# Softmax sums of a pair of slots: multiplied by a constant on VectorE instead of ScalarE

## The chip, the cores and the metric

The kernel runs on one core of a Trainium2 chip. A core has a matrix engine (TensorE, in the profile PE, its weight loads PEld), three engines for element-wise work (VectorE = DVE, ScalarE = ACT, GpSimd = POOL) and a queue for DMA transfers (SyncE = SP). Each engine works through its own instructions in order and waits on semaphores for the others. SBUF is the working memory with 128 partitions, PSUM the small memory into which TensorE writes. The metric is the device time of one execution in microseconds (us), the median of several.

## The reference

The reference is one transformer block with a conditioning vector `c`: a layer norm modulated by `c`, attention over the last 512 positions of a cached K and V, a second modulated layer norm and a gated GELU network.

```python
W = min(4096, max(256, Sk // 4))              # 512
q = (x @ wq).reshape(B, Sq, Hq, Dh)           # 2048 rows, 32 heads of 128
k = k_cache[:, :, Sk - W:, :]                 # 8 heads, each used by 4 heads of q
scores = einsum("bhqd,bhkd->bhqk", q, k) * Dh ** -0.5
p = softmax(scores, axis=-1)
o = einsum("bhqk,bhkd->bhqd", p, v)
A = o.reshape(B, Sq, Hq * Dh) @ wo
x = x + ga * A
x = x + gb * ((gelu(h @ w_gate) * (h @ w_up)) @ w_down)
```

The part that matters here is the softmax: for each row of 512 scores the kernel takes the maximum, the exponentials, their sum, and the exponentials divided by the sum.

## The kernel before

Every matrix operand is held as two float16 halves (a high part and the rest), and every product is three matmuls (`mm3`, its matmuls are line 91), which gives nearly float32 precision from float16 matmuls.

The attention runs first, as 512 slots `t`. A slot is 128 rows of q of one head against the 512 keys. Four slots make a unit (one head, 512 rows). The loop over `t` writes the instructions of every engine in the order in which they are to run; no scheduler changes it. What belongs to one tile of scores is spread over several slots:

- slot t: `scores(t)`, three matmuls into one of two PSUM banks `ps`; `peak(t)` (L1000, VectorE), the negated row maximum `nm`; `expo(t)` (L1009, ScalarE), the exponentials `ee`, with their row sum going to one column of the tile `sm` through a second small instruction that reads the accumulator. `sm` has two columns, one for each slot of a pair (an even slot and the odd one behind it).
- odd slot, behind its `expo`: `recips(t - 1)` (L1014, ScalarE) copies the two sums of the pair, times 1/PSC with PSC = 2**15, into a tile `rr`.
- the even slot after that, behind its `peak` and behind what `run(("e", t))` holds (the low half of a q tile or of an attention output, L754): the inversion `rr = 1/rr` (L1017, VectorE).
- slot t + 2: `high` (L1021, ScalarE), the float16 high half `p` = ee * rr; slot t + 3: `low` (L1026, VectorE), p's low half = ee * rr - high, which reads two tiles of SBUF, and the transposing DMA of both halves into `pt`, from which the product with v (`po`) reads two units later.

The scores of slot t + 2 need the bank `ps` of slot t, so TensorE waits there until `expo(t)` has read it. Between these stand, on TensorE, the projections of q for the next unit (`qa`, `qb`, `qc`, in the first units `pq`), the products with v (`po`) and with wo (`py`). VectorE also adds up q's partial products (L781), makes low halves (L754) and accumulates the output (L970); ScalarE also makes high halves (L753), copies PSUM (L903) and takes sums of squares (L220). GpSimd scales and splits weights (L161, L162, L165, L816 and others). After the 512 slots comes the feed-forward network, in which no softmax stands.

The helper `ts` (L186) is VectorE's tensor_scalar with one operation. All small tiles named here are 128 x 2 or 128 x 1 float32 in SBUF; `ee` is in SBUF in all but 18 of the slots.

Of the kernel before, what the change touches and what calls it, by code (L numbers as in the profile page):

```python
# [14 lines left out]
AF = mybir.ActivationFunctionType  # L15
# [15 lines left out]
PSC = 2.0 ** 15  # L31
# [34 lines left out]
def block_kernel(ctx: ExitStack, tc: tile.TileContext, x, kT, v, wq, wo, wg, wu, wd, cT, wc, wm, out):  # L66
    nc = tc.nc
# [116 lines left out]
    def ts(out, src, a, b=None, op0=ALU.mult, op1=ALU.mult):  # L184
        if b is None:
            nc.vector.tensor_scalar(out, src, a, None, op0=op0)  # L186
        else:
            nc.vector.tensor_scalar(out, src, a, b, op0=op0, op1=op1)  # L188
# [429 lines left out]
    qT, pT, oT, E = {}, {}, {}, {}  # L618
# [392 lines left out]

    def recips(t):
        r = small.tile([P, 2], F32, name="rr", bufs=4)
        nc.scalar.activation(r, E[t]["sm"], AF.Copy, scale=1.0 / PSC)  # L1014
        for k in range(2):
            E[t + k]["r"] = r[:, k:k + 1]
        return lambda: nc.vector.reciprocal(r, r)  # L1017

    def high(t):
        p16 = pool.tile([P, 2, W], F16, tag="p16", name="p16", bufs=NP16)  # L1020
# [553 lines left out]
    with tc.manual_schedule():  # L1574
        begin()
        nexty, invs = [], {}
        for t in range(T + TAIL):
# [21 lines left out]
            if t < T:  # L1599
                expo(t)  # L1600
                if t % 2:
                    invs[t + 1] = recips(t - 1)
# [253 lines left out]
```

## Time and profile before

| | us |
|---|---|
| median of three runs | 1729.17 (1729.11 to 1729.21) |
| profiled execution, its own time | 1728.67 |
| its span, first to last instruction | 1726.9 |

| engine | busy, us | share of the span | instructions |
|---|---|---|---|
| TensorE, matmuls | 1708.5 | 99% | 7999 |
| VectorE | 1425.5 | 83% | 2481 |
| ScalarE | 1256.6 | 73% | 2823 |
| GpSimd | 1089.2 | 63% | 1322 |

A row of a group of instructions reads: line, engine, operation, tiles out and in with their shapes, count; then busy time in us and mean length of one in ns; then the idle time in front of them and what ended it. In the view of one line the three numbers are the shortest, median and longest length in ns. A row of waits reads: who waited for whom, then us in total, number of waits, longest. A row of the timeline reads: start in us from the span's start, length in us, engine, line, operation, tiles; in square brackets stands idle time of the engine in front of it and what ended it. A row of a stretch reads: from and to, its length, then for each engine the busy time and its instructions, TensorE's granted clock as a share of full speed, the DMA share and GB/s. A matmul of 512 columns shows as some 0.38 us, but the next one starts 0.22 us after it, since they overlap.

### The profile page before, as it was taken

The numbers are of one execution on the slowest core, as the hardware profiler recorded it, in microseconds if no ns is written. First come the engines' busy times: TensorE is split into PE (matmuls) and PEld (weight loads), VectorE is DVE, ScalarE is ACT, GpSimd is POOL, SyncE is SP. The second block draws the span as 40 slices with busy tenths as digits, with TensorE's granted clock in tenths as the row PEclk, the third lists the DMA queues.
The fourth block names the chain that finished last, engine by engine and source line by source line (L and its number), as shares of the span: only waits on it lengthen the run. The fifth ranks groups of instructions, "written<-read, shape, count | busy, mean of one in ns | idle before, by whom it ended". The sixth has DMA issues, their size and how long they took to land.

```text
span 1726.9 us, 26328 instructions
## 1 busy us (share of the span) xinstructions
PE 1708.5 (99%) x7999; PEld 784.1 (45%) x8001; DVE 1425.5 (83%) x2481; ACT 1256.6 (73%) x2823; POOL 1089.2 (63%) x1322
## 2 busy tenths in 40 slices
PE   7999999999999999999999999999999999999999
PEld 4444444444444444444444444444444444444444
DVE  8888898988888899888888888888896788676666
ACT  7988788888888877888777777787785354455442
POOL 3879777776788884655665755747760345735424
PEclk9999999999999999999999999999999999999999
DMA  7999999999999998989999999999997555365353
GB/s 245 215 207 214 210 215 199 231 203 223 214 223 225 209 209 182 215 207 228 209 222 223 211 227 209 199 220 222 223 232 163 163 147 192 123 165 174 97 157 104
DMA packets 693454, 343.51 MB, mean 199 GB/s; under 512 B 579136, under 2 KB 602688, under 8 KB 693312
## 3 DMA queue, kind: packets, MB, share of 16 engines
q1 hardware_dynamic: 693024, 341.30, 86.0%
q8 instruction: 63, 1.03, 0.3%
q14 instruction: 79, 0.65, 0.1%
q10 hardware_dynamic: 288, 0.52, 0.1%
HBM read 137.50 MB, written 63.70 MB: 117 GB/s over the span
## 4 chain that ended last, share of the span: by engine, by line
PE 91%; ACT 4%; DVE 3%; DMA 1%; issue 1%; SPq 0%; DVEq 0%; ACTq 0%
PE py L91 19%; PE po L91 17%; PE ps L91 17%; PE qa L91 8%; PE fa L91 8%; PE fc L91 4%; PE qc L91 4%; PE ya L91 3%; PE qb L91 2%; PE fb L91 2%; PE yc L91 2%; ACT ee L1009 1%; PE yb L91 1%; DVE nm L1000 1%; ACT p L1021 1%
## 5 line engine op out<-in xcount | busy, mean ns | idle before, releaser
L1009 ACT ACTIVATE ee<-ps,nm 128x512 f32<-128x512 f32 x512 | 349.6, 683 | 185.4 <-DVE nm L1000 182.6
L1026 DVE SCALAR_TENSOR_TENSOR p<-ee,rr,p 128x512 f16<-128x512 f32 x512 | 457.8, 894 | 8.8 <-ACT p L1021 8.2
L1000 DVE TENSOR_REDUCE nm<-ps 128x1 f32<-128x512 f32 x512 | 349.7, 683 | 94.7 <-PE ps L91 92.5
L91 PE MATMUL ps<-k,qt 128*128 128x512 f16 x1536 | 415.3, 379 | 4.7 <-ACT ee L1009 3.6
L1021 ACT ACTIVATE p<-ee,rr 128x512 f16<-128x512 f32 x512 | 363.9, 711 | 18.8 <-DVE rr L1017 11.6
L91 PE MATMUL po<-pt,v 128*128 128x512 f16 x1536 | 372.9, 379 | 0.7 <-DVE nm L1000 0.7
L91 PE MATMUL py<-wo,ot 128*128 128x512 f16 x1536 | 371.3, 379 | 0.0
L91 PEld LDWEIGHTS <-w 128*128 128x128 f16 x2184 | 213.8, 98 | 260.2 <-issue 2.9
L91 PEld LDWEIGHTS <-v 128*128 128x128 f16 x1536 | 150.1, 98 | 182.4 <-issue 1.6
L91 PEld LDWEIGHTS <-ot 128*128 128x128 f16 x1536 | 150.2, 98 | 181.3
L91 PEld LDWEIGHTS <-qt 128*128 128x128 f16 x1536 | 145.8, 98 | 176.1 <-issue 3.9
L1333 POOL TENSOR_TENSOR fg<-fg 128x512 f32<-128x512 f32 x48 | 63.0, 1312 | 136.0 <-DVE fg L1307 133.1
L754 DVE SCALAR_TENSOR_TENSOR ot<-po,ot 128x512 f16<-128x512 f32 x128 | 87.8, 686 | 41.3 <-ACT ot L753 41.1
L1317 ACT ACTIVATE at<-fg 128x512 f16<-128x512 f32 x92 | 56.4, 626 | 77.2 <-DVE fg L1307 60.7
L1009 ACT ACTIVATION_READ_ACCUMULATOR ee<-ps,nm 128x1 f32 x512 | 100.2, 196 | 0.0
L970 DVE SCALAR_TENSOR_TENSOR acc<-py,ysc,acc 128x512 f32<-128x512 f32 x128 | 94.6, 739 | 5.3 <-PE py L91 5.3
L91 PE MATMUL qa<-t,w 128*128 128x512 f16 x348 | 84.9, 379 | 0.0
L91 PE MATMUL fa<-t,w 128*128 128x512 f16 x336 | 81.6, 379 | 0.1
L237 POOL TENSOR_TENSOR lw<-lw,half__86 128x1 f32<-128x1 f32 x38 | 26.2, 690 | 86.4 <-DVE lw L188 86.3
L404 POOL TENSOR_TENSOR rs<-rs,nhalf 128x1 f32<-128x1 f32 x32 | 18.5, 577 | 93.8 <-DVE rs L398 85.9
L753 ACT ACTIVATE ot<-po 128x512 f16<-128x512 f32 x128 | 73.9, 578 | 5.1 <-PE po L91 5.1
L1703 DVE SCALAR_TENSOR_TENSOR yt<-ya,dyc,yt 128x512 f32<-128x512 f32 x82 | 60.3, 745 | 19.5 <-PE ya L91 19.5
(258 smaller groups left out, 2799.8 us busy)
## 6 DMA issues: line engine op xcount, KB each, us to landing
w<-kept SPq DMA_DIRECT2D x123, 256.0 KB, 3.2
wo<-kept SPq DMA_DIRECT2D x72, 256.0 KB, 3.2
kept<-stage SPq DMA_DIRECT2D x67, 256.0 KB, 3.3
raw<-in_wo SPq DMA_DIRECT2D x56, 256.0 KB, 3.2
kept<-w SPq DMA_DIRECT2D x39, 256.0 KB, 3.4
rw<-in_wq SPq DMA_DIRECT2D x38, 256.0 KB, 3.2
hs<-hf SPq DMA_DIRECT2D x32, 256.0 KB, 2.9
pt<-p SPq DMA_TRANSPOSE x512, 3.5
```

The costliest lines, as they stand in the source:

```text
L91: nc.tensor.matmul(ps, a, b, start=first and n == 0, stop=last and n == 2, skip_group_check=chain)
L237: nc.gpsimd.tensor_tensor(out, out, half_, op=ALU.pow)
L753: nc.scalar.activation(t[:, 0, :], src, AF.Copy, scale=scale)
L754: return lambda: nc.vector.scalar_tensor_tensor(t[:, 1, :], src, scale, t[:, 0, :], op0=ALU.mult, op1=ALU.subtract)
L970: nc.vector.scalar_tensor_tensor(acc[ti], st["p"], by, acc[ti], op0=ALU.mult, op1=ALU.add)
L1000: nc.vector.tensor_reduce(nm, E[t]["ps"], axis=AX.X, op=ALU.max, negate=True)
L1009: nc.scalar.activation(e, E[t]["ps"], AF.Exp, bias=E[t]["nm"], scale=1.0, accum_out=sm[:, t % 2:t % 2 + 1])
L1021: nc.scalar.activation(p16[:, 0, :], E[t]["e"], AF.Copy, scale=E[t]["r"])
L1026: nc.vector.scalar_tensor_tensor(p16[:, 1, :], E[t]["e"], E[t]["r"], p16[:, 0, :], op0=ALU.mult, op1=ALU.subtract)
L1317: nc.scalar.activation(t[:, 0, :], g, AF.Copy)
L1333: nc.gpsimd.tensor_tensor(g[o], g[a], g[b], op=ALU.subtract)
L1703: nc.vector.scalar_tensor_tensor(YT[key], ps, by, YT[key], op0=ALU.mult, op1=ALU.add)
```

## The change

The operation of ScalarE in `recips` goes. In its place, VectorE multiplies the two sums by 1/PSC in front of the inversion, where the inversion stood already.

```diff
     def recips(t):
         r = small.tile([P, 2], F32, name="rr", bufs=4)
-        nc.scalar.activation(r, E[t]["sm"], AF.Copy, scale=1.0 / PSC)
+        sm = E[t]["sm"]
         for k in range(2):
             E[t + k]["r"] = r[:, k:k + 1]
-        return lambda: nc.vector.reciprocal(r, r)
+
+        def inverse():
+            ts(r, sm, 1.0 / PSC)
+            nc.vector.reciprocal(r, r)
+
+        return inverse
```

The lines behind it move by five: `high` is L1026 and `low` L1031 in the kernel after, the inversion L1020. On VectorE, around the slot whose scores start at 664 us in the profile of before (`wmc` and `cols` belong to the modulation by c, `acc`, `ot`, `qt` to the outputs and q), the order before is:

```order
L1000 TENSOR_REDUCE nm<-ps 128x1 [waits PE_49]
L754 SCALAR_TENSOR_TENSOR ot<-po,ot 128x512 [waits Activation_49]
L1017 RECIPROCAL rr<-rr 128x2
L1026 SCALAR_TENSOR_TENSOR p_8674<-ee,rr,p_8674 128x512 [waits DMAHW1_49]
L1000 TENSOR_REDUCE nm<-ps 128x1 [waits PE_49]
L1026 SCALAR_TENSOR_TENSOR p_8703<-ee,rr,p_8703 128x512 [waits DMAHW3_49,Activation_49]
L140 SCALAR_TENSOR_TENSOR wmc,cols<-wmc,sbc 128x512 [waits DMAHW0_49]
L142 TENSOR_SCALAR cols<-cols 128x1 [waits DVE_49]
L1000 TENSOR_REDUCE nm<-ps 128x1 [waits PE_49]
L1017 RECIPROCAL rr<-rr 128x2 [waits Activation_49]
```

The words in brackets are the semaphores that an instruction waits for, by the engine or DMA queue that raises them. After:

```order
L1000 TENSOR_REDUCE nm<-ps 128x1 [waits PE_49]
L754 SCALAR_TENSOR_TENSOR ot<-po,ot 128x512 [waits Activation_49]
L186 TENSOR_SCALAR rr<-sm 128x2
L1020 RECIPROCAL rr<-rr 128x2 [waits DVE_49]
L1031 SCALAR_TENSOR_TENSOR p_8673<-ee,rr,p_8673 128x512 [waits DMAHW1_49]
L1000 TENSOR_REDUCE nm<-ps 128x1 [waits PE_49]
L1031 SCALAR_TENSOR_TENSOR p_8703<-ee,rr,p_8703 128x512 [waits DMAHW3_49,Activation_49]
L140 SCALAR_TENSOR_TENSOR wmc,cols<-wmc,sbc 128x512 [waits DMAHW0_49]
L142 TENSOR_SCALAR cols<-cols 128x1 [waits DVE_49]
L1000 TENSOR_REDUCE nm<-ps 128x1 [waits PE_49]
L186 TENSOR_SCALAR rr<-sm 128x2 [waits Activation_49]
L1020 RECIPROCAL rr<-rr 128x2 [waits DVE_49]
```

In front of each of the 256 inversions stands one more instruction, and the inversion now waits for it, a wait of VectorE on itself. On ScalarE, at the same place, before:

```order
L1009 ACTIVATE ee,sm<-ps,nm 128x512 [waits DVE_49]
L1014 ACTIVATE rr<-sm 128x2 [waits Activation_49]
L1021 ACTIVATE p_8674<-ee,rr 128x512 [waits DMAHW1_49]
L753 ACTIVATE ot<-po 128x512 [waits PE_49]
L1009 ACTIVATE ee,sm<-ps,nm 128x512 [waits DVE_49]
L1021 ACTIVATE p_8703<-ee,rr 128x512 [waits DMAHW3_49,DVE_49]
```

and after:

```order
L1009 ACTIVATE ee,sm<-ps,nm 128x512 [waits DVE_49]
L1026 ACTIVATE p_8673<-ee,rr 128x512 [waits DMAHW1_49,Activation_49]
L753 ACTIVATE ot<-po 128x512 [waits PE_49]
L1009 ACTIVATE ee,sm<-ps,nm 128x512 [waits DVE_49]
L1026 ACTIVATE p_8703<-ee,rr 128x512 [waits DMAHW3_49,DVE_49,Activation_49]
```

The 256 small operations are gone, and each `high` now names a wait of ScalarE on itself too (its source `ee` was written by ScalarE two slots earlier). Nothing else changes its place on any engine or queue.

## Prediction

> **What bounds the kernel now.** I read the page's first part and its chain, then the list of waits, then stretches of the span.
>
> ```profile
> PE 1708.5 (99%) x7999; PEld 784.1 (45%) x8001; DVE 1425.5 (83%) x2481; ACT 1256.6 (73%) x2823; POOL 1089.2 (63%) x1322
> PE 91%; ACT 4%; DVE 3%; DMA 1%; issue 1%; SPq 0%; DVEq 0%; ACTq 0%
> ```
>
> TensorE is busy for 1708.5 of 1726.9 us: all its waits together are 18.4 us. Work added to or taken from another engine reaches the end only where it makes one of these waits longer or shorter, or makes a new one. So the question is how much room VectorE and ScalarE have in front of the scores.
>
> ```profile
> ACT ee L1009 <- DVE nm L1000: 182.6, 233, 2.3
> DVE nm L1000 <- PE ps L91: 92.5, 162, 1.4
> DVE ot L754 <- ACT ot L753: 41.1, 59, 2.6
> ACT p L1021 <- DVE rr L1017: 11.6, 61, 0.3
> PE ps L91 <- ACT ee L1009: 3.6, 6, 1.9
> PE po L91 <- DVE nm L1000: 0.7, 1, 0.7
> ```
>
> The loop of a slot reads from these: VectorE waits for scores (92.5 us), ScalarE waits for VectorE's maximum (182.6 us), TensorE hardly waits for ScalarE (3.6 us). Of the two side engines VectorE is the one that leads: ScalarE has room left and waits for VectorE, not the other way round, and the change moves work from the engine that waits to the one that is waited for. The stretches show where VectorE has least room:
>
> ```profile
> 100.00:200.00 100.00, 100.00 (x472) 45.38 (x470) 86.44 (x153) 81.61 (x195) 83.12 (x111) 1.00 0.96 211
> 640.00:660.00 20.00, 20.00 (x95) 9.04 (x94) 19.77 (x38) 15.04 (x34) 11.81 (x12) 1.00 0.91 207
> 660.00:680.00 20.00, 20.00 (x94) 9.06 (x93) 19.58 (x41) 14.97 (x37) 5.91 (x7) 1.00 0.82 168
> 680.00:700.00 20.00, 20.00 (x97) 9.52 (x96) 19.05 (x38) 14.98 (x35) 12.91 (x12) 1.00 0.86 177
> 60.00:80.00 20.00, 17.54 (x81) 7.52 (x80) 16.80 (x33) 18.87 (x45) 16.53 (x22) 1.00 0.99 214
> 80.00:100.00 20.00, 18.50 (x78) 7.88 (x78) 17.02 (x31) 17.94 (x46) 13.10 (x14) 0.91 1.05 207
> ```
>
> In an ordinary stretch (100 to 200) VectorE is idle for 13.56 of 100 us. From 640 to 700 it is idle for 0.23 + 0.42 + 0.95 = 1.60 of 60 us, and TensorE still runs without a gap: this is the place with nothing left. From 60 to 100 TensorE already waits (2.46 and 1.50 us) and ScalarE, at 18.87 of 20, is the fuller one.
>
> **The change, part by part.** Removed: 256 operations of ScalarE. What one takes from its queue is read from an odd slot (with it) and an even one (without):
>
> ```profile
> 77.84 0.19 ACT L1009 ACTIVATION_READ_ACCUMULATOR ee<-ps,nm 128x1 f32 x1
> 78.06 0.20 ACT L1014 ACTIVATE rr<-sm 128x2 f32<-128x2 f32 x1
> 78.17 0.67 ACT L1021 ACTIVATE p<-ee,rr 128x512 f16<-128x512 f32 x1
> ...
> 80.50 0.20 ACT L1009 ACTIVATION_READ_ACCUMULATOR ee<-ps,nm 128x1 f32 x1
> 80.59 0.69 ACT L1021 ACTIVATE p<-ee,rr 128x512 f16<-128x512 f32 x1
> ```
>
> From the read of the sum to `high` it is 78.17 - 77.84 = 0.33 us with the operation and 80.59 - 80.50 = 0.09 without: 0.24 us of ScalarE's queue for each pair, 256 x 0.24 = 61 us in all. The added self-wait of `high` costs nothing that I can see: what it waits for is two slots old, and the even `high` above already carries two waits and starts 0.09 us behind its neighbour.
>
> Added: 256 multiplications on VectorE, each followed by an inversion that waits for it. A chain of such small dependent steps stands in the trace:
>
> ```profile
> L398 DVE TENSOR_SCALAR rs<-mv x32: 153/153/155, 5.3 to 1353.5; 128x1 f32<-128x1 f32 x32
> 703.70 0.18 DVE L396 BATCH_NORM_AGGREGATE mv<-bn 128x2 f32<-128x6 f32 x1
> 703.92 0.15 DVE L398 TENSOR_SCALAR rs<-mv 128x1 f32<-128x1 f32 x1
> 703.99 0.68 DVE L1000 TENSOR_REDUCE nm<-ps 128x1 f32<-128x512 f32 x1
> ```
>
> L398 waits for L396 and starts 703.92 - 703.70 - 0.18 = 0.04 us behind its end; the next instruction, which waits for nothing on VectorE, starts 0.07 us after L398's start. So an instruction that someone on the same engine waits for costs its full length and 0.04 us: 0.153 + 0.04 = 0.19 us for each pair, 49 us in all.
>
> That price holds when nobody disturbs the multiplication. Whether GpSimd does, no row of before shows for this shape, but there are neighbours on both sides:
>
> ```profile
> L1026 DVE SCALAR_TENSOR_TENSOR p<-ee,rr,p x512: 722/746/1835, 34.4 to 1323.8; 128x512 f16<-128x512 f32 x171
> L1026 DVE SCALAR_TENSOR_TENSOR p<-ee,rr,p 128x512 f16<-128x512 f32 x512 | 457.8, 894 | 8.8 <-ACT p L1021 8.2
> L509 DVE TENSOR_SCALAR xs<-xs,mv,rs 128x512 f32<-128x512 f32 x8 | 4.3, 539 | 2.3 <-POOL rs L404 2.3
> L1000 DVE TENSOR_REDUCE nm<-ps 128x1 f32<-128x512 f32 x512 | 349.7, 683 | 94.7 <-PE ps L91 92.5
> 74.25 1.16 POOL L162 TENSOR_TENSOR wo<-wor,wo 128x512 f16<-128x512 f32 x1
> 74.41 1.55 DVE L1026 SCALAR_TENSOR_TENSOR p<-ee,rr,p 128x512 f16<-128x512 f32 x1
> ```
>
> `low` takes 746 ns at the median and up to 1835. The long one at 74.41 runs beside a GpSimd operation that ends at 75.41, and ends 75.96 - 75.41 = 0.55 us after it: it stood until GpSimd was through. L509, a tensor_scalar from SBUF to SBUF, does 512 columns in 539 ns where L1000 needs 683, so between tiles of SBUF this operation moves its columns faster than an ordinary one, and what it uses for that it may have to share with GpSimd, as `low` does. The added multiplication is the same operation, SBUF to SBUF with two columns. The bounds are therefore 0 (L398, one column, never longer than 155 ns) and 1835 - 722 = 1.11 us (the longest `low`). I take the mean excess of `low`, 894 - 746 = 0.15 us, because `low` stands right behind the inversion in most pairs and meets GpSimd in the same state. That makes 0.19 + 0.15 = 0.34 us for each pair.
>
> [...]
>
> What reaches the end, place by place:
>
> ```profile
> 640.00:700.00 60.00, 1.84 (x12) 1.00 0.87 184
> 662.77 0.69 ACT L1009 ACTIVATE ee<-ps,nm 128x512 f32<-128x512 f32 x1 [1.34 <-DVE nm L1000]
> 664.08 0.81 PE L91 MATMUL ps<-k,qt 128*128 128x512 f16 x3
> 62.34 0.82 PE L91 MATMUL ps<-k,qt 128*128 128x512 f16 x3 [0.95 <-ACT ee L1009]
> 80.75 1.36 PE L91 MATMUL ps<-k,qt 128*128 128x512 f16 x3 [1.86 <-ACT ee L1009]
> 59.00:81.00 22.00, 1.02 (x5) 1.00 0.98 214
> 736.34 0.81 PE L91 MATMUL ps<-k,qt 128*128 128x512 f16 x3 [0.20 <-ACT ee L1009]
> 1131.10 0.81 PE L91 MATMUL ps<-k,qt 128*128 128x512 f16 x3 [0.18 <-ACT ee L1009]
> ```
>
> - 640 to 700: the first row counts L1017 alone, 12 inversions. They bring 12 x 0.34 = 4.1 us to a VectorE with 1.6 us idle, so it falls 2.5 us behind. The scores at 664.08 start 0.62 us after the exponentials that they need end (663.46); that much is swallowed, 1.9 us become waits of TensorE.
> - 60 to 100: the wait at 62.34 ends with a full ScalarE, which is rid of 0.24 us. The chain to 80.75 runs over one removed operation (78.06) and, before that, over VectorE with two inversions: 2 x 0.34 - 0.24 = +0.44. Sum +0.2 us. The low clock behind this wait, (1 - 0.91) x 20 = 1.8 us at 80 to 100, stays.
> - Elsewhere (510 to 620, 720 to 800, and single slots to 1260) the room is VectorE's idle time, 13.56 us in 100 with 20 pairs or 6.8 us added, so on the mean it suffices. It fails where the scores already start at once, as at 736.34 and 1131.10. In 32 of 510 slots they start less than 0.7 us after their exponentials end (for each slot: the scores' start minus the end of the exponentials two slots before, 0.14 at the least). If half of a pair's 0.34 - 0.24 + 0.15 = 0.25 us is paid in half of these, it is 16 x 0.12 = 2 us.
> - Waits on GpSimd come in lumps of up to 1.11 us, not as means; for lumps that exceed the room in these slots I add 1 us.
>
> Sum: 1.9 + 0.2 + 2 + 1 = 5.1 us. The profiled execution took 1728.67, so 1733.8; the median of the runs is 0.5 us higher: 1734.3 us, 0.3% slower. ScalarE's 61 us count for almost nothing, since it waits for VectorE in the places that matter.
>
> **The rivals.** (1) The multiplication meets no one: 0.19 us a pair. At 640 to 700 it is 12 x 0.19 = 2.3 against 1.6, 0.7 us behind, swallowed but for 0.1; at 60 to 100 it is 2 x 0.19 - 2 x 0.24 = -0.1; elsewhere ScalarE's 0.24 pays for it. The time stays at 1729.2, give or take 1. For it speaks that L398 never grew; against it that L398 has one column. (2) The other side, faster: ScalarE is the bound from 59 to 81, with five of the removed operations in it (the row 59 to 81 above counts L1014 alone). If each gives 0.24, 1.2 us of the waits of 0.95 and 1.86 go, and with the shorter wait the clock may stay up, 1.8 more: 1729.2 - 3.0 = 1726.2, and another 0.5 from the three late waits of 0.2 makes 1725.7. This decides only if a pair costs VectorE less than 0.24 us; the VectorE steps in the chain to 80.75 speak against it. (3) VectorE cannot make up the lumps: a multiplication waits for one GpSimd operation, the next one gets in between, and `low` waits for that one too. Then a pair costs 0.34 and another 0.15, and VectorE, with 20 x 0.49 = 9.8 of 13.56 us filled in an ordinary stretch, has lost its reserve in every crowded one: three times the sum, +15 us, 1744.
>
> **How the numbers follow.** The measurement can tell about 0.2% (3.5 us) from no change. The forecast, with costs on GpSimd between a third and twice the sum (1730.5 to 1739): 0.50, of which 0.12 end within 0.2%. Rival 1: 0.32, of which 0.02 end slower. Rival 2: 0.06, of which 0.04 are beyond 0.2%. Rival 3: 0.12, all slower. Faster 0.04; slower 0.38 + 0.02 + 0.12 = 0.52; same 0.44. The range leaves out most of rival 2 and the far half of rival 3: 1728.2 to 1744. The likeliest case's own range is 1730.5 to 1739.
>
> **What would show it.** Right: the multiplication's row has a median near 150 ns and a longest one of 0.6 us or more beside GpSimd operations; TensorE's wait "ps <- ACT ee" grows from 3.6 to 7 us or more, with new ones at 655 to 700; "ACT p <- DVE rr" grows from 11.6. Wrong: all 256 stay under 0.17 us, or VectorE's idle time at 640 to 700 is not used up. The prediction falls if `low` gets shorter by what the multiplication waits, so that the two share one wait.

## The result, and the profile after

The changed kernel takes 1758.87 us, the median of five runs (1758.27 to 1760.36), beside 1729.14 for the kernel before on the same chip. The ratio is 1.0177 (95% interval 1.0166 to 1.0188): slower by 1.8%, 30 us. The forecast was 1734.3 with a range up to 1744; the direction was right, the size was not, and the time lies outside the range.

The page of the kernel after, first its busy times, then two groups of instructions (in the rows of one line the three numbers are shortest, median and longest in ns):

```profile
PE 1715.3 (98%) x7999; PEld 782.6 (45%) x8001; DVE 1521.3 (87%) x2737; ACT 1214.9 (69%) x2567; POOL 1074.8 (61%) x1322
L1031 DVE SCALAR_TENSOR_TENSOR p<-ee,rr,p 128x512 f16<-128x512 f32 x512 | 473.3, 924 | 2.4 <-ACT p L1026 1.9
L1020 DVE RECIPROCAL rr<-rr 128x2 f32<-128x2 f32 x256 | 42.4, 166 | 8.8
L186 DVE TENSOR_SCALAR rr<-sm x256: 149/176/1205, 29.5 to 1349.6; 128x2 f32<-128x2 f32 x128
```

VectorE gained 1521.3 - 1425.5 = 95.8 us of busy time. The multiplication takes 149 ns undisturbed and up to 1205; 111 of the 256 are above 300 ns and 38 above 600 (counted in the timeline), and all of them together lie 50.6 us above 0.153 us apiece. `low` grew from 894 to 924 ns on the mean, the inversion from 154 to 166, and it waits 8.8 us for the multiplication. ScalarE lost 1256.6 - 1214.9 = 41.7 us.

The waits after come first, then two of before that the prediction did not show (us in total, number, longest; "issue" is time for which the profile shows no releaser):

```profile
ACT p L1026 <- ACT ee L1009: 62.4, 120, 1.0
DVE ot L754 <- ACT ot L753: 41.0, 69, 2.3
DVE nm L1000 <- PE ps L91: 30.2, 47, 1.4
DVE qt L754 <- ACT qt L753: 26.3, 93, 1.2
PE ps L91 <- ACT ee L1009: 19.2, 30, 1.4
PEld L91 <- issue: 43.9, 71, 1.7
```

```profile
DVE qt L754 <- ACT qt L753: 23.6, 69, 1.4
PEld L91 <- issue: 9.1, 24, 1.2
```

TensorE waits for exponentials 19.2 us instead of 3.6, and VectorE's wait for scores, its real reserve, went from 92.5 to 30.2. VectorE still stands at L754 for ScalarE's L753 as long as before (41.0 + 26.3 against 41.1 + 23.6). The first row is new, and its releaser is wrong: the exponentials of two slots earlier had ended at least 2.8 us before. In the timeline 168 of the 256 even `high`s start 0.08 to 0.09 us behind the end of the inversion, so that is what they wait for; the kernel `old_r` below bears it out.

How TensorE loses shows best in the number of its matmuls, since a short gap hides behind matmuls whose shown ends overlap. The same stretch, first before, then after:

```profile
300.00:400.00 100.00, 100.00 (x477) 46.19 (x475) 87.84 (x165) 84.48 (x210) 74.33 (x103) 1.00 1.02 219
```

```profile
300.00:400.00 100.00, 96.50 (x453) 43.75 (x452) 93.11 (x176) 77.81 (x179) 73.25 (x98) 1.00 0.92 203
```

There are 453 matmuls instead of 477, 5% fewer, at the same granted clock of 1.00, with VectorE at 93.11 instead of 87.84. One case from this stretch, in the timeline of after:

```profile
303.50 0.68 DVE L1000 TENSOR_REDUCE nm<-ps 128x1 f32<-128x512 f32 x1
304.10 0.68 DVE L754 SCALAR_TENSOR_TENSOR ot<-po,ot 128x512 f16<-128x512 f32 x1
304.60 1.27 POOL L663 TENSOR_TENSOR raw<-raw,gs 128x512 f32<-128x512 f32 x1
304.70 1.20 DVE L186 TENSOR_SCALAR rr<-sm 128x2 f32<-128x2 f32 x1
305.43 0.81 PE L91 MATMUL ps<-k,qt 128*128 128x512 f16 x3
305.93 0.17 DVE L1020 RECIPROCAL rr<-rr 128x2 f32<-128x2 f32 x1
305.96 0.62 POOL L161 TENSOR_SCALAR wo<-raw 128x512 f16<-128x512 f32 x1
306.01 1.10 DVE L1031 SCALAR_TENSOR_TENSOR p<-ee,rr,p 128x512 f16<-128x512 f32 x1
307.04 0.68 DVE L1000 TENSOR_REDUCE nm<-ps 128x1 f32<-128x512 f32 x1
307.89 0.68 ACT L1009 ACTIVATE ee<-ps,nm 128x512 f32<-128x512 f32 x1
308.71 0.81 PE L91 MATMUL ps<-k,qt 128*128 128x512 f16 x3 [0.54 <-ACT ee L1009]
```

GpSimd's L663 begins 0.10 us ahead of the multiplication, and the multiplication ends at 305.90, 0.03 us behind L663's end at 305.87: 1.20 us for two columns. While the inversion runs, GpSimd starts L161 at 305.96, 0.05 us ahead of `low`, and `low` takes 1.10 us. The scores that end at 306.24 get their maximum only at 307.04, 0.80 us late; the exponentials follow at 307.89, 0.17 us behind the maximum's end since ScalarE has other work in front of them, and TensorE's next scores wait 0.54 us. This is the chain of rival 3.

The other multiplications of the profile after behave alike: each of the 111 that take more than 300 ns ends 20 to 27 ns behind the end of an instruction of GpSimd, and of the 82 that start while no instruction of GpSimd runs the longest takes 170 ns.

Where the 30 us come from, by place. For each of the 512 maxima (L1000) the start in a profile minus the start of the same maximum in the profile of before; the table gives how much this delay grew between two borders in the time of before (the last three columns are kernels of the experiments):

| us of before | after | `swap` | `onecol` | `fill4` |
|---|---|---|---|---|
| 0 to 100 | 0.5 | -0.3 | -0.7 | 0.2 |
| 100 to 500 | 13.2 | 5.1 | 1.6 | 6.7 |
| 500 to 640 | 8.0 | 1.0 | -0.1 | 3.0 |
| 640 to 700 | 2.4 | 2.9 | 2.8 | 6.5 |
| 700 to 1100 | 0.4 | -1.0 | -0.7 | 3.8 |
| 1100 to the last | 5.7 | -0.5 | 0.3 | 4.6 |
| all | 30.2 | 7.3 | 3.3 | 24.8 |

The whole loss lies in the attention, and 21.2 of the 30.2 us in the stretches from 100 to 640. Where the 5.7 us behind 1100 come from is not shown by any run.

### The profile page after: what moved, and what is told of

Its sections match the earlier page's. It is cut to its first block, busy times and chain, and to the rows that moved or that the text cites. A ratio compares the mean times of both kernels' runs of the same rounds, so it can differ in the third digit from the quotient of the medians.

```text
span 1757.1 us, 26629 instructions
## 1 busy us (share of the span) xinstructions
PE 1715.3 (98%) x7999; PEld 782.6 (45%) x8001; DVE 1521.3 (87%) x2737; ACT 1214.9 (69%) x2567; POOL 1074.8 (61%) x1322
## 5 line engine op out<-in xcount | busy, mean ns | idle before, releaser
L1031 DVE SCALAR_TENSOR_TENSOR p<-ee,rr,p 128x512 f16<-128x512 f32 x512 | 473.3, 924 | 2.4 <-ACT p L1026 1.9
L91 PE MATMUL ps<-k,qt 128*128 128x512 f16 x1536 | 414.7, 379 | 21.3 <-ACT ee L1009 19.2
L1026 ACT ACTIVATE p<-ee,rr 128x512 f16<-128x512 f32 x512 | 366.0, 715 | 86.8 <-ACT ee L1009 62.4
L1000 DVE TENSOR_REDUCE nm<-ps 128x1 f32<-128x512 f32 x512 | 347.9, 680 | 31.0 <-PE ps L91 30.2
L754 DVE SCALAR_TENSOR_TENSOR ot<-po,ot 128x512 f16<-128x512 f32 x128 | 87.8, 686 | 41.4 <-ACT ot L753 41.0
L186 DVE TENSOR_SCALAR rr<-sm 128x2 f32<-128x2 f32 x256 | 89.8, 351 | 0.1
L753 ACT ACTIVATE ot<-po 128x512 f16<-128x512 f32 x128 | 74.9, 585 | 5.1 <-PE po L91 5.1
```

The source lines that it names most:

```text
L91: nc.tensor.matmul(ps, a, b, start=first and n == 0, stop=last and n == 2, skip_group_check=chain)
L753: nc.scalar.activation(t[:, 0, :], src, AF.Copy, scale=scale)
L754: return lambda: nc.vector.scalar_tensor_tensor(t[:, 1, :], src, scale, t[:, 0, :], op0=ALU.mult, op1=ALU.subtract)
L1000: nc.vector.tensor_reduce(nm, E[t]["ps"], axis=AX.X, op=ALU.max, negate=True)
L1026: nc.scalar.activation(p16[:, 0, :], E[t]["e"], AF.Copy, scale=E[t]["r"])
L1031: nc.vector.scalar_tensor_tensor(p16[:, 1, :], E[t]["e"], E[t]["r"], p16[:, 0, :], op0=ALU.mult, op1=ALU.subtract)
```

## The experiments

The expectations name theories by letters. Theory A is the price of the prediction: a two-column multiplication waits for GpSimd. The others are told where they are put to the test. Each diff is against the kernel after, where nothing else is said.

**Is it the wait for GpSimd?** `onecol` does the same multiplication one column at a time:

```diff
-            ts(r, sm, 1.0 / PSC)
+            for k in range(2):
+                ts(r[:, k:k + 1], sm[:, k:k + 1], 1.0 / PSC)
             nc.vector.reciprocal(r, r)
```

> The multiplication as two instructions of one column each, then the inversion of both columns; one instruction more on VectorE for each pair than in the kernel after, and two more than before. Theory A (the two-column multiplication waits for GpSimd, a one-column one doesn't, as L398's row): the multiplications' longest stays below 0.2 us, VectorE is charged about 0.26 us a pair instead of 0.39 on the mean, ScalarE's waits for the inversion fall from 79 to 20 us, and the time falls back to 1730 to 1736. Theory B (the mere extra dependent step of 0.19 us on a full VectorE costs the 30 us): one more instruction makes it worse than after, 1760 or more.

Measured: 1732.64 us, ratio to before 1.0022 (1.0013 to 1.0032). The line of the multiplications, the group of `low`, and TensorE's wait:

```profile
L186 DVE TENSOR_SCALAR rr<-sm x512: 133/143/155, 30.1 to 1322.7; 128x1 f32<-128x1 f32 x171
L1032 DVE SCALAR_TENSOR_TENSOR p<-ee,rr,p 128x512 f16<-128x512 f32 x512 | 457.9, 894 | 3.5 <-ACT p L1027 3.2
PE ps L91 <- ACT ee L1009: 5.0, 10, 1.6
```

None of the 512 one-column multiplications takes more than 155 ns, though 363 of them start while an instruction of GpSimd runs (174 of the 256 two-column ones do in the change), and `low` is back at 894 ns. One thing that was expected did not come: ScalarE's `high`s still stand 46.7 + 3.5 = 50.2 us for the inversion by the waits, not 20 (the larger part is put down to ScalarE itself, as in the first row of after), and the time is back all the same. With twice as many instructions, 26 of the 30 us are gone. So the wait of the two-column form for GpSimd is the cause without which the loss does not come about.

`nomul` inverts the sums directly and leaves the constant out:

```diff
-            ts(r, sm, 1.0 / PSC)
-            nc.vector.reciprocal(r, r)
+            nc.vector.reciprocal(r, sm)
```

> Leaves out the multiplication by the constant altogether: the inversion reads the sums themselves, no operation of ScalarE and none of VectorE is in its place (p comes out smaller by the constant). Shows what the removal on ScalarE alone is worth. Both theories: 1725 to 1729, a gain of at most 3 us where ScalarE is full (60 to 100 us of the span), since TensorE's waits for ScalarE are 3.6 us before.

Measured: 1726.51 us, ratio 0.9988 (0.9979 to 0.9998). Taking the operation off ScalarE without adding anything is worth some 2 us in this kernel (0.3 to 3.6 by the interval).

The next three put the multiplication into a tile that nobody reads, in front of the inversion. `dummy2` and `dummy1` are against the kernel before, with ScalarE's operation kept, in the two-column and the one-column form:

```diff
-        return lambda: nc.vector.reciprocal(r, r)
+        sm, d = E[t]["sm"], small.tile([P, 2], F32, name="rd", bufs=4)
+
+        def inverse():
+            ts(d, sm, 1.0 / PSC)          # dummy1: ts(d[:, 0:1], sm[:, 0:1], 1.0 / PSC)
+            nc.vector.reciprocal(r, r)
+
+        return inverse
```

> The kernel before, with its operation of ScalarE, and one multiplication of the two sums (128x2) into a tile that nobody reads, on VectorE in front of each inversion; nothing waits for it. Theory A: it waits for GpSimd as in the kernel after (mean some 350 ns, longest over 1 us) and the time is 1750 to 1765. Theory B (the dependent step costs): without anyone waiting for it, it costs 0.07 us a pair and the time stays below 1733.

> As the run with a two-column multiplication that nobody reads, but with one column of the sums (128x1). Theory A: no wait for GpSimd, length 145 to 155 ns throughout, 0.07 us a pair, time 1729 to 1732. Theory B: the same as with two columns, within 1 us.

Measured: `dummy2` 1738.2 us, ratio 1.0058 (1.0043 to 1.0073); `dummy1` 1729.97, ratio 1.0009 (1.0000 to 1.0018). `dummy1` is where theory A had it. `dummy2` lies between the two theories' windows and fits neither: its multiplication waits nearly as long as in the change (mean 337 ns), so theory B is out, but that wait alone costs 9 us, not 30. Something must come on top. `dummy2_noact` does the same in the kernel after (the inversion reads the sums themselves, so the constant is left out):

```diff
-            ts(r, sm, 1.0 / PSC)
-            nc.vector.reciprocal(r, r)
+            ts(d, sm, 1.0 / PSC)
+            nc.vector.reciprocal(r, sm)
```

> The kernel after, except that nobody waits for the two-column multiplication: it writes a tile that nobody reads, and the inversion reads the sums themselves (the constant is left out, p comes out smaller). Against the kernel after it lacks only the dependence of the inversion on the multiplication. If the waits for GpSimd alone make the loss: 1755 or more. If the dependent step behind a multiplication that waits makes a large part of it (the next GpSimd operation gets in ahead of low): 1733 to 1740, some 2 us under the run with the same multiplication and ScalarE's operation kept (1738.2), and low's mean stays near 860 ns in place of 924.

Measured: 1733.05 us, ratio 1.0023 (1.0013 to 1.0033). Its busy times and its `low`:

```profile
PE 1710.0 (99%) x8001; PEld 783.3 (45%) x8001; DVE 1466.3 (85%) x2737; ACT 1217.8 (70%) x2567; POOL 1107.7 (64%) x1322
L1033 DVE SCALAR_TENSOR_TENSOR p<-ee,rr,p 128x512 f16<-128x512 f32 x512 | 430.0, 840 | 4.0 <-ACT p L1028 3.6
```

Here the multiplication waits for GpSimd as much as in the change (mean 365 ns against 351), yet VectorE has 1521.3 - 1466.3 = 55.0 us less to do, and the time is 25.8 us shorter. Most of the difference is `low`: 840 ns instead of 924. Without a dependent step between them, multiplication and `low` share one wait for GpSimd here; where the inversion has to wait for the multiplication, GpSimd begins its next operation and `low` waits once more, 2 x (0.924 - 0.840) = 0.17 us for each pair, 43 us in all. In the change, behind 103 of the 111 multiplications of more than 300 ns, an instruction of GpSimd that began between 0.08 us ahead of the multiplication's end and 0.11 us behind it is running when `low` starts; in the other 8 pairs `low` takes at most 751 ns. The timelines show it pair by pair: behind a multiplication of more than 300 ns the next `low` takes 1162 ns on the mean in the change (111 pairs) and 810 in `dummy2_noact` (115 pairs); behind the shorter ones it takes 871 and 834. So the change is dear through two things together: the two-column form, and the dependent step behind it.

**Is it `high`, standing for the inversion?** Theory C: ScalarE's even `high`s, which now stand 79 us in all for the late inversion (62.4 + 11.2 + 4.9 by the waits), hold up the exponentials behind them. Theory D: VectorE is simply full, and the waits of ScalarE are only a sign of it. In `old_r`, `high` and `low` take the inverted sums of the pair before, so nothing waits for the new ones; VectorE's order and work stay. The softmax is divided by another pair's sums there.

```diff
+        before_.append(r)
         for k in range(2):
-            E[t + k]["r"] = r[:, k:k + 1]
+            E[t + k]["r"] = before_[max(0, len(before_) - 2)][:, k:k + 1]
```

> The kernel after, except that high and low of a pair use the inverted sums of the pair before it, which have long been there (the softmax is divided by the wrong pair's sums). VectorE does the same instructions in the same order, the dependent step included; only ScalarE's high no longer waits for this slot's inversion. Theory C: the waits of high for the inversion are gone and the time is 1731 to 1738. Theory D: VectorE is as full as before, 1752 to 1762.

Measured: 1761.85 us, ratio 1.0182 (1.0168 to 1.0195), no gain at all, where theory D had it. The only wait of `high` left, and TensorE's:

```profile
ACT p L1029 <- DMA pt<-p: 7.6, 10, 2.1
PE ps L91 <- ACT ee L1009: 17.8, 28, 1.5
```

Theory C falls: the standing of `high` is a symptom. That it went with the dependence also shows what it was, whatever releaser the row of after names.

**What was ScalarE's relief worth?** `actdummy` puts an operation of the same size back on ScalarE at the old place, into a tile that nobody reads:

```diff
+        nc.scalar.activation(d, sm, AF.Copy, scale=1.0 / PSC)
```

> The kernel after, with an operation of ScalarE at the place and of the size of the removed one, writing a tile that nobody reads: the VectorE part of the change alone. Theory D: what the removal gave ScalarE is worth little, 1757 to 1762. If ScalarE's relief paid a part of the cost, the time rises further, to 1765 or more.

Measured: 1777.42 us, ratio 1.0279 (1.0264 to 1.0294), 18.5 us over the change; theory D had expected the relief to be worth little.

```profile
DVE nm L1000 <- PE ps L91: 15.8, 24, 1.2
DVE ot L754 <- ACT ot L753: 59.5, 75, 2.4
DVE qt L754 <- ACT qt L753: 47.6, 112, 1.4
```

The operation makes ScalarE's L753 later, and VectorE stands at L754 for 107.1 us instead of 67.3. So the relief on ScalarE was worth 18.5 us once VectorE was full, though only some 2 in `nomul`, where VectorE has room.

**Does the place count?** `swap` moves multiplication and inversion in front of L754, directly behind the maximum; `bswap` does the same in the kernel before, `onecol_swap` in `onecol`.

```diff
-            run(("e", t))
             inv()
+            run(("e", t))
```

> The kernel after with the multiplication and the inversion issued directly behind the maximum, in front of the low half of a q or output tile (L754) that stands between them in most even slots; nothing else moves. Theory C (the inversion comes too late for ScalarE's high, which stands 79 us for it in the kernel after, and this makes the loss): the waits of high for the inversion fall to 30 us or less and the time to 1740 or less. Theory D (VectorE is simply full, with 0.45 us more to do for each pair, and a wait of ScalarE is only its sign): high waits less, but the time stays at 1752 to 1762.

> The kernel before with its inversion directly behind the maximum. ScalarE's high waits only 11.6 us for it in the kernel before, and TensorE 3.6 us for ScalarE: 1727 to 1730, the same within 0.2%.

> Both cures together, with nothing left out: two one-column multiplications and the inversion, all directly behind the maximum. Theory C with A: neither a wait for GpSimd nor one of high is left, 1726 to 1730, no slower than before. If a VectorE that has 0.26 us more to do for each pair costs by itself: 1731 to 1733.

Measured: `swap` 1735.24 us, ratio 1.0035 (1.0022 to 1.0048); `bswap` 1728.33, ratio 0.9995 (0.9987 to 1.0004); `onecol_swap` 1730.17, ratio 1.0006 (0.9997 to 1.0015). Of `swap`:

```profile
L186 DVE TENSOR_SCALAR rr<-sm x256: 149/159/1204, 29.9 to 1325.0; 128x2 f32<-128x2 f32 x128
L1031 DVE SCALAR_TENSOR_TENSOR p<-ee,rr,p 128x512 f16<-128x512 f32 x512 | 471.1, 920 | 4.3 <-ACT p L1026 3.9
DVE ot L754 <- ACT ot L753: 14.5, 33, 1.9
DVE qt L754 <- ACT qt L753: 9.2, 34, 1.0
DVE nm L1000 <- PE ps L91: 56.4, 102, 2.0
```

The multiplication still waits up to 1204 ns, `low` takes 920, VectorE is busy for 1508.6 us, nearly as in the change; yet 23.6 of the 30 us are gone. (`low` takes 920 ns in `onecol_swap` too, where no multiplication takes more than 155 ns, so behind L754 its length is not the second wait.) The time and the waits of `high` (3.0 us) are those of theory C's window, but `old_r` has ruled its cause out. VectorE stands at L754 for 23.7 us instead of 67.3: it now does the new work, and waits for GpSimd, while the source of L754 is still being made by ScalarE. So for the maxima the sum of two things counts, VectorE's work and its standing for L753. `bswap` stays within its window; `onecol_swap` falls between its two.

**Only the amount, or also the lumps?** Theory F: that sum sets the time, however the work comes. Theory L: the single long waits for GpSimd do. `fill1` to `fill4` add one to four more one-column multiplications per pair to `onecol`, into a tile that nobody reads; none of them takes over 155 ns. `fill2_swap` and `fill4_swap` put the same in front of L754.

```diff
+            for k in range(4):          # 1, 2, 3 or 4; in fill1, fill2 with sm[:, k:k + 1]
+                ts(d[:, k:k + 1], sm[:, 0:1], 1.0 / PSC)
             for k in range(2):
                 ts(r[:, k:k + 1], sm[:, k:k + 1], 1.0 / PSC)
             nc.vector.reciprocal(r, r)
```

> The kernel with two one-column multiplications (1732.6 us, VectorE busy 1473.7), with one more one-column multiplication per pair into a tile that nobody reads, in front of them: about 256 x 0.14 = 36 us more work for VectorE in even pieces, 1510 busy, close to the 1521 of the change (1758.9 us). Theory F (any such amount of work in this place costs as much): 1745 to 1755. Theory L (the single long waits for GpSimd make the loss): 1734 to 1738.

> The same with two more one-column multiplications per pair, VectorE busy about 1546, 25 more than in the change. Theory F: 1765 or more. Theory L: 1738 to 1745.

> fill2 with its four multiplications and the inversion directly behind the maximum, in front of L754. Theory F: at least 15 us under fill2, since VectorE does the work while it would stand at L754 waiting for ScalarE. Theory L: within 5 us of fill2, since even pieces of work are cheap in both places.

> Three more one-column multiplications per pair than in onecol, all in the place of the change. From fill1 to fill2 the sum of VectorE's busy time and of its standing at L754 grew from 1543 to 1566, so here about 1589, as in the change. Theory F (this sum sets the time, however the work comes): 1752 to 1762. Theory L (the long single waits for GpSimd do): 1744 to 1748, the step of 6 us from fill1 to fill2 once more.

> Four more per pair, the sum about 1612. Theory F: 1768 to 1780, beside the kernel with the extra operation of ScalarE (sum 1618, 1777.4). Theory L: 1750 to 1756.

> fill4 with multiplications and inversion in front of L754. From onecol_swap to fill2_swap the sum grew from 1504 to 1525, so here about 1548. Theory F: 1736 to 1741, 30 us or more under fill4. Theory L: 1739 to 1745, some 10 us under fill4.

Measured, with the kernels above in the order of the sum (VectorE's busy time from each page, the two waits at L754 added, and what VectorE still waits for scores; span of the profiled execution):

| kernel | busy | at L754 | sum | waits for scores | span | median |
|---|---|---|---|---|---|---|
| `nomul` | 1420.4 | 36.4 | 1456.8 | 124.3 | 1724.3 | 1726.51 |
| `bswap` | 1428.9 | 49.4 | 1478.3 | 101.3 | 1726.5 | 1728.33 |
| before | 1425.5 | 64.7 | 1490.2 | 92.5 | 1726.9 | 1729.14 |
| `onecol_swap` | 1483.7 | 20.4 | 1504.1 | 77.8 | 1727.4 | 1730.17 |
| `dummy1` | 1440.2 | 68.9 | 1509.1 | 75.8 | 1728.1 | 1729.97 |
| `dummy2_noact` | 1466.3 | 54.2 | 1520.5 | 74.3 | 1732.5 | 1733.05 |
| `fill2_swap` | 1506.6 | 18.7 | 1525.3 | 62.3 | 1732.6 | 1733.73 |
| `onecol` | 1473.7 | 53.7 | 1527.4 | 57.6 | 1730.1 | 1732.64 |
| `swap` | 1508.6 | 23.7 | 1532.3 | 56.4 | 1734.2 | 1735.24 |
| `fill1` | 1486.4 | 57.0 | 1543.4 | 48.1 | 1733.0 | 1734.81 |
| `fill4_swap` | 1536.5 | 12.6 | 1549.1 | 42.3 | 1735.6 | 1736.86 |
| `dummy2` | 1463.7 | 85.9 | 1549.6 | 51.9 | 1738.4 | 1738.2 |
| `fill2` | 1501.8 | 64.6 | 1566.4 | 32.2 | 1739.5 | 1740.98 |
| `fill3` | 1511.8 | 71.5 | 1583.3 | 21.1 | 1744.3 | 1746.53 |
| after | 1521.3 | 67.3 | 1588.6 | 30.2 | 1757.1 | 1758.87 |
| `old_r` | 1522.5 | 67.2 | 1589.7 | 29.5 | 1756.5 | 1761.85 |
| `fill4` | 1522.7 | 78.2 | 1600.9 | 11.5 | 1751.4 | 1753.43 |
| `actdummy` | 1511.3 | 107.1 | 1618.4 | 15.8 | 1775.5 | 1777.42 |

```profile
PE 1715.0 (98%) x8001; PEld 781.9 (45%) x8001; DVE 1522.7 (87%) x4017; ACT 1214.6 (69%) x2567; POOL 1088.2 (62%) x1322
L186 DVE TENSOR_SCALAR rr<-sm x512: 134/143/149, 30.0 to 1344.5; 128x1 f32<-128x1 f32 x171
DVE nm L1000 <- PE ps L91: 11.5, 20, 1.7
```

(The rows are those of `fill4`.) `fill1`, `fill2`, `fill3` and `fill4` came out as theory L had it, and missed theory F's windows. For `fill1` and `fill2` that says little, since the work that F counted on did not come (1510 and 1546 us of busy time were expected, 1486.4 and 1501.8 measured), and `fill3` too stayed 6 us under its expected sum. `fill4` is the clear case, with a larger sum than the change and a shorter time: VectorE as busy as in the change (1522.7) costs 24.5 us of span when the work comes in even pieces, with hardly any reserve left (11.5 us of waits for scores), while the change loses 30.2 with 30.2 us of reserve unused. With the place it is the other way round: `fill4_swap` lies in theory F's window of 1736 to 1741 and 2 us below the other's, though it is 16.6 us under `fill4` where F had 30, and `fill2_swap` is 7.3 us under `fill2`, between the two (at least 15, at most 5). So neither holds alone: the sum matters also for even work, less steeply than F had it, and the lumps come on top. Estimated from `fill3` and `fill4`, even work with the sum of the change would end at 1744.3 + (1588.6 - 1583.3) x 7.1 / 17.6 = 1746.4: about 19.5 of the 30.2 us are the price of a full VectorE, and about 10.7 that of the lumps, which leave reserve unused in one slot and exceed it in another. The split is rough: by the table of places the change loses 11.5 us more than `fill4` from 100 to 640 and 7.5 less from 640 to 1100. One place shows the lumps: the eight slots that start at 285 us of before lose 2.0 us in the change (the case shown above lies there) and 0.0 in `fill4`. From 285 to 326, two groups of eight, it is 2.1 and 0.5.

The sum includes the standing at L754, which itself grows when the loop is late; it orders most of the kernels (not `fill4` beside the change), but it is not a cause apart from them.

**A kernel that beats both.** The constant need not be multiplied at all. `psc1` is `nomul` with 2^15 put into a constant by which the product with v is scaled anyway, so that it computes the whole block; `psc1_swap` has the inversion in front of L754 as well.

```diff
-ACC = 2.0 ** -14
+ACC = 2.0
...
-            ts(r, sm, 1.0 / PSC)
-            nc.vector.reciprocal(r, r)
+            nc.vector.reciprocal(r, sm)
```

> A version meant to beat both: the inversion reads the sums themselves, no multiplication and no operation of ScalarE, and the constant goes into the constant by which the product with v is scaled already (2 in place of 2**-14), so the output's scale is kept; small p lose bits of their low half. Time as in the run without a multiplication: 1725.5 to 1727.5.

> The version without a multiplication (the constant moved into the scale of the product with v), with the inversion directly behind the maximum. high's remaining waits for the inversion (some 10 us) go; since TensorE waits only 3 us for ScalarE there, 1725 to 1727, no more than 1 us from the version without this move.

Measured: `psc1` 1726.6 us, ratio 0.9984 (0.9974 to 0.9994); `psc1_swap` 1726.88, ratio 0.9985 (0.9976 to 0.9994). Both are a little faster than before, by 0.15%, and the place adds nothing where VectorE has room.

## Why the prediction was wrong

- **What bounds the kernel, and the direction:** right. TensorE is full, VectorE leads the loop, and the work went from the engine that waits to the one that is waited for.
- **The price of a pair, 0.34 us:** nearly right. VectorE's busy time grew by 95.8 us and its wait on itself is 8.8, together 104.6 / 256 = 0.41 us. The multiplication itself has 0.351 (0.153 + 0.15 = 0.30 was put down), the self-wait 0.034 (0.04). What was missing is `low`, for which the sum had no change; it grew by 0.03 us each. By place one price for all pairs was wrong. The first two rows are stretches of before (the fifth engine is GpSimd), the others the multiplications of the same slots in the profile of after:

```profile
500.00:640.00 140.00, 140.00 (x658) 63.80 (x657) 122.76 (x212) 113.97 (x272) 120.58 (x141) 1.00 1.00 217
640.00:700.00 60.00, 60.00 (x283) 27.61 (x282) 58.41 (x115) 44.99 (x103) 30.63 (x31) 1.00 0.87 184
L186 DVE TENSOR_SCALAR rr<-sm x28: 151/455/1205, 514.6 to 657.3; 128x2 f32<-128x2 f32 x28
L186 DVE TENSOR_SCALAR rr<-sm x12: 152/158/610, 663.5 to 720.9; 128x2 f32<-128x2 f32 x12
```

Where GpSimd is busy for 120.58 of 140 us, the median multiplication takes 455 ns; where it is busy for 30.63 of 60, 158 ns. VectorE is fullest where GpSimd has least to do.

- **Where the reserve is exceeded:** 640 to 700 was put at 1.9 us and lost 2.4; 60 to 100 at 0.2, and the table has 0.5 from 0 to 100. That the first comes near is luck in part: its 4.1 us held 12 x 0.15 = 1.8 us of waits for GpSimd, which hardly came there, and `onecol`, in which no multiplication waits, loses 2.8 us in the same place.
- **The step that failed is "Elsewhere", the sentence that "on the mean it suffices", with its 2 us and the 1 us for lumps.** Measured elsewhere: 30.2 - 2.4 - 0.5 = 27.3 us. It counted all of VectorE's idle time, 13.56 us in 100, as room. But an idle time is room only where the new work can go into it. Of the waits of before, 41.1 + 23.6 = 64.7 us are VectorE standing at L754 for ScalarE, and the new work was put behind L754; the room was the 92.5 us of waits for scores alone, and 256 x 0.34 = 87 us would nearly have filled it by the forecast's own price. One of the two rows (41.1) stood in the prediction and was not set against the sum. `swap` shows the reading: in front of L754 the same work costs 6.1 us. Nor is the room spread evenly. Of the waits of before, the first row is from 100 to 200 us, the stretch that the forecast took for ordinary, the second from 200 to 300, the last three from 500 to 640:

```profile
DVE nm L1000 <- PE ps L91: 11.2, 21, 1.2
DVE nm L1000 <- PE ps L91: 4.3, 9, 0.8
DVE ot L754 <- ACT ot L753: 6.0, 8, 0.9
DVE nm L1000 <- PE ps L91: 3.8, 8, 0.7
DVE qt L754 <- ACT qt L753: 3.5, 11, 0.6
```

From 500 to 640, 28 pairs bring 28 x 0.34 = 9.5 us even by the forecast's price to 3.8 us of room, and the change lost 8.0 us there; from 200 to 300 it lost 6.2.

- **The lumps:** rival 3 had the mechanism, "the next one gets in between, and low waits for that one too", and the timeline and `dummy2_noact` show it. Its price, 0.49 us a pair against 0.41 measured, was not too low; what failed is its step from there to the time, "three times the sum", again for want of the right room. It got 0.12 where it was the case that came about, and 1744 where it was 1759.
- **The condition under which the prediction was to fall**, that multiplication and `low` share one wait, holds in `dummy2_noact` (`low` 840 ns) and not in the change (924). I had not seen that the dependence of the inversion decides between the two.
- **ScalarE's 61 us "count for almost nothing":** wrong at this load. They were worth 18.5 us (`actdummy`), through L753 and VectorE's standing at L754. Without them the change would have cost 48 us.
- **What was to show it:** the multiplication's median is 176 ns and its longest 1205, TensorE's wait 19.2 us, and the wait of `high` grew, under another releaser's name. Rival 1 (it meets no one) is wrong for two columns and right for one (`onecol`); rival 2 is ruled out.

## What to carry to other kernels

Before adding work to the engine that leads a loop, split its idle time by what ends it, and count as room only the waits that stand behind the place of the new work; a wait for another engine in front of that place is no room, but becomes some if the work is moved ahead of it. A tiny operation that is seen to wait for GpSimd should be written in a form that does not (here one column at a time: at most 155 ns in `onecol`, up to 1205 with two columns), above all when the next instruction depends on it: with that dependence `low` took 924 ns on the mean here, without it 840. Best of all, a constant factor goes into a scale that is applied anyway (`psc1`, 1726.6 us).

## What the runs showed of the hardware

- The same tensor_scalar from SBUF to SBUF takes 149 to 1205 ns with two columns of float32 (after) and 133 to 155 ns with one (`onecol`), beside the same GpSimd work: 351 ns on the mean for two columns at once, 142 for each of the two instructions of one column.
- In the change and `dummy2_noact`, multiplication and `low` shared the wait for GpSimd where no dependence stood between them, and paid it twice where one did: behind a multiplication of more than 300 ns the next `low` has 810 ns on the mean without the dependence (`dummy2_noact`) and 1162 with it.
- Independent small operations on VectorE cost less than their length here: from `fill1` to `fill4`, 3 x 256 instructions of 143 ns add 1522.7 - 1486.4 = 36.3 us of busy time, 0.05 us each.
